# Windowed attention with sink keys, then a gated feed-forward layer: loads paced by use, more DMA transposes, and a fixed place for the sink-key copies

## The chip, the cores and the metric

The kernel runs on one core of one Trainium2 chip. The time is device microseconds (us) of one execution; of seven runs of the kernel before, the median is 254.44 us (253.92 to 255.36). The profile is of one execution; its times are counted from the start of its span.

## The reference

There are 4 batches of 8 heads, 768 positions and 64 elements a head. Each position attends to the 4 sink keys at the start and to the last 128 positions. The attention output, as 3072 rows of 512 elements, goes through a row normalisation and a gated feed-forward layer of width 1536.

```python
scores = scale * np.matmul(q, k.transpose(0, 1, 3, 2))
keep = is_sink | ((rel >= 0) & (rel < window))
a = softmax(np.where(keep, scores, -1e9))
x = np.matmul(a, v)                       # then rows of all heads side by side
xn = x / np.sqrt(np.mean(x * x, -1) + 1e-6) * rms_g
g = xn @ w_gate
out = (g * sigmoid(g) * (xn @ w_val)) @ w_out
```

## The kernel before

**Tiles.** The rows are cut into 24 blocks of 128 (NB), 6 to a batch. A block g of batch b and place t in the batch has q, k and v of all heads as bf16 tiles of 128x512, cast from fp32 by the DMA that loads them (`load_q`, `load_k`, `load_v`, issued by POOL, lines 111 and 124). q and k are then transposed into `QKT[b]`, a tile for a whole batch of which there are two. This is done either on PE (eight 128x128 transposes into PSUM, line 251, and a copy by ACT or DVE, lines 264 and 286), or by two DMA transposes issued by SP (line 278). Before, the DMA does it for blocks 13 to 17 and 19 to 23.

**One block's attention.** `unit_s(g)` makes the scores of the keys of block g with the queries of blocks g and g+1 (line 413; in the last block of a batch with its own alone), so it needs k of block g and q of g and g+1. ACT takes the exponential (line 422), and the mask is a multiplication on DVE (line 388) or, in batches 2 and 3 outside their first block, two selections on POOL (lines 390 and 395). `unit_sink(b)` prepares the sink keys of a batch: it clears a tile, copies 4 columns of the transposed k twice (64 partitions by 16 elements each, line 297, on DVE), and makes the sink values (lines 306 and 310). `unit_sink_scores` uses the copies (line 321) two blocks at a time. `unit_av(g, u)` multiplies by v for four heads (lines 444 to 456); DVE takes the reciprocal of the sums (line 479) and scales the output (line 484, `unit_norm`); ACT squares it (line 494); DVE works out the row factor (lines 503 to 525) and the scaled row (line 541). From block 8 on, the rows are transposed by a DMA of SP (line 549), before that on PE (line 563).

**Feed-forward.** Four blocks make a group G of 512 rows; there are six groups. For each of 12 slices of the width there is a gate product and a value product (line 581, four matmuls of 128x512 each), a tanh on ACT (line 594) and two DVE operations (lines 599 and 607). Then each block has 12 output matmuls (line 622), a copy by ACT (line 629) and a store by SP (line 631).

**Order.** The feed-forward parts of a group are woven with the attention units of the blocks ahead. `step(g)` gives four slots: the scores of g in slot 0, the output of g-1 in slots 1 and 3, the transposes in slot 2 (of block g+2 on PE, or of g+3 by DMA). `manual_schedule` makes the order in which the code is written binding for the engines that it names: in the main part PE and SP. For the others, a planner in the compiler sets the order from its own estimate of costs and readiness. All engines take their instructions in order. `tc.issue_after(ins)` puts the instructions of its block behind `ins` on the engine of `ins`; it adds no wait between engines.

**Loads.** POOL issues all loads: at first, in an order written out by hand, the weights and blocks 1 to 7, and then, behind the last of the weights, blocks 8 to 23. The pool `ld` has 18 buffers for q and 18 for k; v has a place of its own for every block. All PSUM tiles of the main part share eight banks.

Of the kernel before, what the change touches and what calls it, by code (L numbers as in the profile page):

```python
# [28 lines left out]
def kernel(  # L29
# [13 lines left out]
    nc = tc.nc  # L43
# [12 lines left out]
    GB = 4  # L56
# [6 lines left out]
    NEG = -32768.0  # L63
    RMS_EPS = 1e-6 * RSQRT_SCALE ** 2
    MS_SCALE = RSQRT_SCALE / math.sqrt(DM)
    DMA_T_FROM = 12

    DMA_X_FROM = 8
    FA = 10
    WEAVE_FROM = 9  # L70
    POOL_MASK_FROM = 2
    MANUAL = {mybir.EngineType.PE, mybir.EngineType.SP}
    MANUAL_ALL = MANUAL | {mybir.EngineType.Activation, mybir.EngineType.DVE}

    const = ctx.enter_context(tc.tile_pool(name="const", bufs=1))
    ld = ctx.enter_context(tc.tile_pool(name="ld", bufs=3 * NT))
    vld = ctx.enter_context(tc.tile_pool(name="vld", bufs=B))
    qkt = ctx.enter_context(tc.tile_pool(name="qkt", bufs=2))
    sink = ctx.enter_context(tc.tile_pool(name="sink", bufs=2))
# [36 lines left out]
    def load_q(g):  # L116
        QS[g] = load_block(q, "qs", g)

    def load_k(g):
        KS_[g] = load_block(k, "ks", g)  # L120

    def load_v(g):
        b, t = divmod(g, NT)
        nc.gpsimd.dma_start(  # L124
            out=V16[b][:, t, :, 0:D],
            in_=v[b, :, t * P:(t + 1) * P, :].rearrange("h t d -> t h d"),
        )
# [12 lines left out]
    def load_wo(c):  # L140
        rows = slice(c * FTN // 2, (c + 1) * FTN // 2)
        return nc.gpsimd.dma_start(out=wo[:, rows, :], in_=wo_src[:, rows, :]).ins
# [41 lines left out]
    with tc.manual_schedule(engines={mybir.EngineType.Pool, mybir.EngineType.DVE}):  # L184
        load_q(1)
        nc.gpsimd.affine_select(
            out=ident, in_=ident, compare_op=ALU.not_equal, fill=1.0,
            base=0, pattern=[[-1, P]], channel_multiplier=1,
        )
        nc.gpsimd.affine_select(  # L190
            out=amasks[:, 1, 0, :], in_=amasks[:, 1, 0, :], compare_op=ALU.is_ge,
            fill=NEG, base=0, pattern=[[1, P]], channel_multiplier=-1,
        )
        nc.vector.tensor_scalar(
            out=amasks[:, 1, 1, :], in0=amasks[:, 1, 0, :], scalar1=-1.0, scalar2=NEG,
            op0=ALU.mult, op1=ALU.add,
        )
        nc.vector.tensor_copy(out=amasks[:, 0, :, :], in_=amasks[:, 1, :, :])
        nc.vector.memset(amasks[0:NS, 0, :, :], 0.0)
        unit_cast(0)  # L200
        unit_cast(1)
        load_k(1)
        load_v(0)
        load_v(1)
        load_w(0)
        load_q(2)
        load_k(2)
        load_w(1)
        load_q(3)
        load_v(2)  # L210
        load_k(3)
        load_v(3)
        nc.gpsimd.affine_select(
            out=sel[:, 0:H * NS].rearrange("p (h s) -> p h s", s=NS),
            in_=sel[:, 0:H * NS].rearrange("p (h s) -> p h s", s=NS),
            compare_op=ALU.not_equal, fill=1.0,
            base=0, pattern=[[0, H], [-1, NS]], channel_multiplier=1,
        )
        nc.gpsimd.affine_select(
            out=headm, in_=headm, compare_op=ALU.is_ge, fill=0.0,  # L220
            base=0, pattern=[[-NS, H]], channel_multiplier=1,
        )
        nc.gpsimd.affine_select(
            out=headm, in_=headm, compare_op=ALU.is_ge, fill=0.0,
            base=NS - 1, pattern=[[NS, H]], channel_multiplier=-1,
        )
        load_w(2)
        load_w(3)
        load_q(4)
        load_w(4)  # L230
        load_k(4)
        load_w(5)
        load_v(4)
        for g in range(GB + 1, 2 * GB):
            load_q(g)
            load_k(g)
            load_v(g)
        load_wo(0)
        last_load = load_wo(1)
    with tc.issue_after(last_load):  # L240
        for g in range(2 * GB, NB):
            load_q(g)
            load_k(g)
            load_v(g)


    QKT, KSK, VSK, ESK, E, X16, MS, XR, XNT = {}, {}, {}, {}, {}, {}, {}, {}, {}
# [8 lines left out]
    def unit_t1(g, i):  # L256
# [9 lines left out]
            in_=ps[:, 0:HP * P].rearrange("p (x c) -> p x c", c=P),  # L266
        )

    def by_dma(g):
        return g >= DMA_T_FROM and g % NT > 0  # L270

    def unit_t(g):
        b, t = divmod(g, NT)
# [17 lines left out]
    def unit_sink(b):  # L291
        ks = sink.tile([P, HP * KSW], BF16, name="ksk")
        nc.vector.memset(ks, 0.0)
        ksv = ks.rearrange("p (h c) -> p h c", c=KSW)
        for hi in range(2):
            pr = slice(hi * D, (hi + 1) * D)
            nc.vector.tensor_copy(
                out=ksv[pr, :, hi * NS:(hi + 1) * NS],
                in_=QKT[b][pr, 1, :, 0:NS],
            )  # L300
        KSK[b] = ks
        vs = sink.tile([P, H, VW], BF16, name="vsk")
        for half in range(2):
            ps = pp[0].tile([P, 512], FP32, name="pvs", tag="b1")
            hs = slice(half * 4, half * 4 + 4)
            nc.tensor.matmul(
                out=ps[:, 0:HW], lhsT=sel, rhs=V16[b][:, 0, hs, :],
                start=True, stop=True,
            )
            nc.vector.tensor_tensor(  # L310
                out=vs[:, hs, :], in0=ps[:, 0:HW].rearrange("p (h c) -> p h c", c=VW),
                in1=headm[:, hs].unsqueeze(2).to_broadcast((P, 4, VW)), op=ALU.mult,
            )
        VSK[b] = vs
# [153 lines left out]
        if u == 1 and g >= 2:  # L468
            unit_rms(g)

    PV, RDEN = {}, {}

    def heads_of(g, u):

# [6 lines left out]
    def unit_norm(g, u, pvv):  # L481
        if (g, u) not in RDEN:
            unit_recip(g, u, pvv)
        nc.vector.tensor_tensor(  # L484
            out=X16[g][:, heads_of(g, u), :], in0=pvv[:, :, 0:D],
            in1=RDEN.pop((g, u)).unsqueeze(2).to_broadcast((P, 4, D)), op=ALU.mult,
        )

    def unit_sq(g, u):
        if u == 0:  # L490
# [145 lines left out]
    def step(g):  # L636


        b, t = divmod(g, NT)
        slots = [[], [], [], []]  # L640
        if g < NB:
            slots[0].append(lambda: unit_s(g))
            if t == 1:
                slots[1].append(lambda: unit_sink(b))
            if t in (2, 4):
                slots[1].append(lambda: unit_sink_scores(b, t))
        if g <= NB:
            slots[1].append(lambda: unit_av(g - 1, 0))
            slots[3].append(lambda: unit_av(g - 1, 1))
        if g - 3 < NB:  # L650
            slots[0].append(lambda: unit_x(g - 3))
        if g + 2 < NB and not by_dma(g + 2):
            slots[2 if t != 5 else 1].append(lambda: unit_t(g + 2))
        if g + 3 < NB and by_dma(g + 3):
            slots[2].append(lambda: unit_t(g + 3))
        return slots

    def weave(parts, slots, upto=0, first=False):
# [54 lines left out]

    with tc.manual_schedule(engines=MANUAL):


        fa, fb = [], []
        for ft in range(0, FA, 2):
            fa += parts_f(0, (ft, ft + 1), slice(0, GN // 2))
            fb += parts_f(0, (ft, ft + 1), slice(GN // 2, GN))  # L720
        for ft in range(FA, FTN):
            fb += parts_f(0, (ft,), slice(0, GN))
        weave(fa, [
            [lambda: unit_t1(2, 1), lambda: unit_bias(1, 1), lambda: unit_sp(1, 1), lambda: unit_sink(0)],
            [lambda: unit_t1(3, 0), lambda: unit_s(2)],
            [lambda: unit_sink_scores(0, 2)],
            [lambda: unit_t1(3, 1), lambda: unit_bias(3, 0), lambda: unit_av(2, 0), lambda: unit_sp(3, 0), lambda: unit_av(2, 1)],
            [lambda: unit_av(3, 0)],
            [lambda: unit_av(3, 1), lambda: unit_t1(4, 0)],
            [lambda: unit_bias(3, 1), lambda: unit_sp(3, 1)],  # L730
            [lambda: unit_x(2)],
            [lambda: unit_t1(4, 1)],
            [lambda: unit_x(3)],
        ], first=True)
        slots = [[lambda: unit_t1(5, 0)], [lambda: unit_t1(5, 1)], [lambda: unit_s(4)], [lambda: unit_sink_scores(0, 4)], [lambda: unit_t(6)], []]
        for g in range(5, NB + 3):
            slots += step(g)
        slots[6].pop()
        slots[10].pop()
        outs = []  # L740
        n = 0
        for G in range(NG):

            parts = fb if G == 0 else []
            for ft in range(FTN if G > 0 else 0):
                parts += parts_f(G, (ft,), slice(0, GN))
                if ft % 3 == 2 and outs:
                    parts += outs.pop(0)
            outs = [parts_o(G, tb) for tb in range(GB)]
            if G < WEAVE_FROM or G == NG - 1:  # L750
                for o in outs:
                    parts = parts + o
                outs = []
            n1 = 6 + 4 * ((G + 2) * GB + 2 - 5) + 1
            weave(parts, slots[n:n1], 1)
            n = n1
# [33 lines left out]
```

The softmax here doesn't subtract the row's maximum and nothing guards it: scores larger than these inputs give would overflow.

## Time and profile before

| | |
|---|---|
| median of 7 runs | 254.44 us |
| profiled execution, its time / its span | 254.44 / 252.7 us |
| PE busy | 240.4 us |
| DVE busy | 181.2 us |
| ACT busy | 139.4 us |
| POOL busy | 98.0 us |
| DMA packets / bytes | 105849 / 25.74 MB |
| loads of q, k, v: issue to landing, median | 7.7 to 7.8 us |
| DMA transposes, issue to landing, median | 2.4 us |

How to read it: the shares of the engines say how busy each was over the span; in the row of 40 slices, one digit is the busy share of 6.3 us in tenths. The chain of waits is followed back from the last instruction, at each step to what released it. A timeline row has start and duration in us, the engine, the line, the operation, output and inputs; in brackets the idle time of the engine before it and what ended it. Matmuls overlap, so their pitch (start to start) says what they cost and not their duration.

### The profile page before, as it was taken

The numbers are of one execution on the slowest core, as the hardware profiler recorded it, in microseconds if no ns is written. First come the engines' busy times: TensorE is split into PE (matmuls) and PEld (weight loads), VectorE is DVE, ScalarE is ACT, GpSimd is POOL, SyncE is SP. The second block draws the span as 40 slices with busy tenths as digits, with TensorE's granted clock in tenths as the row PEclk, the third lists the DMA queues.
The fourth block names the chain that finished last, engine by engine and source line by source line (L and its number), as shares of the span: only waits on it lengthen the run. The fifth ranks groups of instructions, "written<-read, shape, count | busy, mean of one in ns | idle before, by whom it ended". The sixth has DMA issues, their size and how long they took to land.

```text
span 252.7 us, 4804 instructions
## 1 busy us (share of the span) xinstructions
PE 240.4 (95%) x1733; PEld 128.5 (51%) x1760; DVE 181.2 (72%) x474; ACT 139.4 (55%) x312; POOL 98.0 (39%) x129
## 2 busy tenths in 40 slices
PE   5988989999999999999999999999999999999994
PEld 1436868855555444454454454454454544444441
DVE  5474897899778999539989459988359992287700
ACT  2576768789896365556473546466545441323211
POOL 8987779289985652134041004044201000000000
PEclk9999999999999999999999999999999999999999
DMA  9999999999999999750120550320421013200022
GB/s 128 150 171 191 188 157 189 185 155 151 179 198 171 150 127 150 125 172 18 21 52 14 145 145 3 64 56 18 117 84 23 0 21 95 94 0 0 0 86 83
DMA packets 105849, 25.74 MB, mean 102 GB/s; under 512 B 95073, under 2 KB 102753, under 8 KB 105826
## 3 DMA queue, kind: packets, MB, share of 16 engines
q0 software_dynamic: 80704, 13.90, 76.1%
q1 hardware_dynamic: 24082, 11.28, 18.9%
q10 hardware_dynamic: 1040, 0.26, 0.5%
q8 instruction: 14, 0.23, 0.4%
q14 instruction: 9, 0.07, 0.1%
HBM read 28.31 MB, written 6.29 MB: 137 GB/s over the span
## 4 chain that ended last, share of the span: by engine, by line
PE 79%; DVE 13%; ACT 4%; issue 2%; DMA 2%; ACTq 0%; DVEq 0%
PE po L622 24%; PE pg L581 20%; PE pvl L581 20%; PE pT L413 3%; DVE hT L607 3%; DVE p L599 3%; PE pv L456 2%; PE pqk L251 2%; DVE et L388 2%; PE pv L452 2%; DMA osb<-in_q_dram 2%; DVE xr L541 2%; PE pv L444 1%; ACT et L422 1%; PE pss L321 1%
## 5 line engine op out<-in xcount | busy, mean ns | idle before, releaser
L581 PE MATMUL pg<-xnt,wg 128*128 128x512 bf16 (+1 forms) x317 | 73.5, 352 | 1.4 <-ACT xnt L567 0.7
L581 PE MATMUL pvl<-xnt,wv 128*128 128x512 bf16 (+1 forms) x322 | 73.4, 353 | 0.3
L622 PE MATMUL po<-wo,hT 128*128 128x512 bf16 x279 | 64.9, 379 | 0.5 <-issue 0.2
L594 ACT ACTIVATE th<-pg 128x512 bf16<-128x512 f32 x72 | 42.9, 596 | 38.4 <-PE pg L581 38.4
L599 DVE SCALAR_TENSOR_TENSOR p<-th,pg 128x512 bf16<-128x512 bf16 x72 | 49.0, 680 | 20.0 <-ACT th L594 19.6
L607 DVE TENSOR_TENSOR hT<-p,pvl 128x512 bf16<-128x512 bf16 x72 | 49.3, 685 | 3.7 <-PE pg L581 0.5
L581 PEld LDWEIGHTS <-wg 128*128 128x128 bf16 x328 | 30.5, 98 | 27.4 <-issue 1.4
L581 PEld LDWEIGHTS <-wv 128*128 128x128 bf16 x328 | 30.4, 98 | 27.1 <-issue 1.1
L422 ACT ACTIVATE et<-pT 128x512 bf16<-128x512 f32 x76 | 39.7, 601 | 4.9 <-PE pT L413 4.7
L390 POOL TENSOR_SCALAR_AFFINE_SELECT et<-et 128x512 bf16<-128x512 bf16 x20 | 13.1, 658 | 74.2 <-ACT et L422 74.2
L622 PEld LDWEIGHTS <-hT 128*128 128x128 bf16 x288 | 26.6, 98 | 29.8 <-issue 0.8
L494 ACT ACTIVATE sq<-x 128x256 bf16<-128x256 bf16 x48 | 20.0, 417 | 27.1 <-DVE x L484 26.8
L629 ACT ACTIVATE osb<-po 128x512 f32<-128x512 f32 x24 | 14.4, 602 | 25.8 <-PE po L622 20.8
L111 POOL DMA_DIRECT2D ks<-in_k_dram x23 | 20.5, 891 | 8.2 <-DMA wo<-in_moe_w_out_dram 2.8
L111 POOL DMA_DIRECT2D qs<-in_q_dram x23 | 20.6, 897 | 7.7 <-PE pv L456 2.6
L124 POOL DMA_DIRECT2D v<-in_v_dram x24 | 21.5, 895 | 2.3 <-DMA wg<-in_moe_w_gate_dram 1.4
L484 DVE TENSOR_TENSOR x<-pv,rden 128x256 bf16<-128x256 f32 x48 | 20.2, 422 | 0.8
L541 DVE SCALAR_TENSOR_TENSOR xr<-x,y,gb 128x512 bf16<-128x512 bf16 (+1 forms) x25 | 19.9, 798 | 0.7
L479 DVE RECIPROCAL rden<-pv 128x4 f32<-128x4 f32 x48 | 8.4, 176 | 16.1 <-PE pv L456 15.9
L388 DVE TENSOR_TENSOR et<-et,masks 128x1024 bf16<-128x1024 bf16 (+1 forms) x22 | 13.8, 638 | 2.7 <-ACT et L422 2.7
L456 PE MATMUL pv<-v,et 128*128 128x65 bf16 x168 | 15.3, 193 | 0.0
L452 PE MATMUL pv<-v,et 128*128 128x65 bf16 x136 | 12.7, 193 | 0.0
(75 smaller groups left out, 217.0 us busy)
## 6 DMA issues: line engine op xcount, KB each, us to landing
out_dram<-osb SPq DMA_DIRECT2D x24, 256.0 KB, 2.1
v<-in_v_dram POOLq DMA_DIRECT2D x24, 128.0 KB, 7.8
qs<-in_q_dram POOLq DMA_DIRECT2D x23, 128.0 KB, 7.7
ks<-in_k_dram POOLq DMA_DIRECT2D x23, 128.0 KB, 7.7
wg<-in_moe_w_gate_dram POOLq DMA_DIRECT2D x6, 256.0 KB, 7.7
wv<-in_moe_w_val_dram POOLq DMA_DIRECT2D x6, 256.0 KB, 8.0
wo<-in_moe_w_out_dram POOLq DMA_DIRECT2D x2, 768.0 KB, 10.4
osb<-in_k_dram ACTq DMA_DIRECT2D x1, 256.0 KB, 4.8
```

Of the source, the lines that this page charges most:

```text
L111: nc.gpsimd.dma_start(out=tl, in_=src[b, :, t * P:(t + 1) * P, :].rearrange("h t d -> t h d"),)
L124: nc.gpsimd.dma_start(out=V16[b][:, t, :, 0:D], in_=v[b, :, t * P:(t + 1) * P, :].rearrange("h t d -> t h d"),)
L422: nc.scalar.activation(out=et[:, hi].rearrange("p j n c -> p (j n c)"), in_=banks[u][hi], func=ACT.Exp, scale=inv_sqrt_d,)
L456: nc.tensor.matmul(out=dest, lhsT=E[(g, h, 0)], rhs=V16[b][:, t, h, :], start=(t == 0), stop=True, skip_group_check=True,)
L484: nc.vector.tensor_tensor(out=X16[g][:, heads_of(g, u), :], in0=pvv[:, :, 0:D], in1=RDEN.pop((g, u)).unsqueeze(2).to_broadcast((P, 4, D)), ...
L494: nc.scalar.activation(out=sq, in_=xh, func=ACT.Square, scale=MS_SCALE, accum_out=MS[g][:, u:u + 1],)
L541: nc.vector.scalar_tensor_tensor(out=XR[g][-1], in0=x16[:, c], scalar=y[:, 4:5], in1=gb[:, c], op0=ALU.mult, op1=ALU.mult,)
L581: nc.tensor.matmul(out=ps[:, i * n:(i + 1) * n], lhsT=w_sb[:, kt, ft * P:(ft + 1) * P], rhs=XNT[G][:, kt, cols], start=(kt == 0), stop=(kt ...
L594: nc.scalar.activation(out=st["th"], in_=st["pg"], func=ACT.Tanh, scale=0.5)
L599: nc.vector.scalar_tensor_tensor(out=p1, in0=st["th"], scalar=1.0, in1=st["pg"], op0=ALU.add, op1=ALU.mult,)
L607: nc.vector.tensor_tensor(out=HT[key][:, i:i + n, cols], in0=p1.rearrange("p (n c) -> p n c", n=n), in1=pvl.rearrange("p (n c) -> p n c", ...
L622: nc.tensor.matmul(out=st["po"], lhsT=HT[(G, ft // 2)][:, ft % 2, tb * P:(tb + 1) * P], rhs=wo[:, ft, :], start=(ft == 0), stop=(ft == FTN ...
```

## The change

Three things are changed. The pool `ld` has 4 buffers each for q and k in place of 18, and POOL's order is now bound to the code as well: the loads of block g+6 stand in slot 2 of step g, those of blocks 8, 9 and 10 in the slots before step 5. The DMA transposes start at block 10 and take the first block of a batch too, so blocks 10, 11, 12 and 18 leave PE and ACT. The two copies of the sink keys are put behind the `unit_norm` written last before them.

```diff
-    DMA_T_FROM = 12
+    DMA_T_FROM = 10
+    LD = 4
+    AHEAD = 6
-    MANUAL = {mybir.EngineType.PE, mybir.EngineType.SP}
+    MANUAL = {mybir.EngineType.PE, mybir.EngineType.SP, mybir.EngineType.Pool}
-    ld = ctx.enter_context(tc.tile_pool(name="ld", bufs=3 * NT))
+    ld = ctx.enter_context(tc.tile_pool(name="ld", bufs=LD))
...
-        last_load = load_wo(1)
-    with tc.issue_after(last_load):
-        for g in range(2 * GB, NB):
-            load_q(g)
-            load_k(g)
-            load_v(g)
+        load_wo(1)
...
+    def unit_load(g):
+        load_q(g)
+        load_k(g)
+        load_v(g)
...
     def by_dma(g):
-        return g >= DMA_T_FROM and g % NT > 0
+        return g >= DMA_T_FROM
...
-        for hi in range(2):
-            pr = slice(hi * D, (hi + 1) * D)
-            nc.vector.tensor_copy(
+        with tc.issue_after(LAST[0]):
+            for hi in range(2):
+                pr = slice(hi * D, (hi + 1) * D)
+                nc.vector.tensor_copy(
...
-        nc.vector.tensor_tensor(
+        LAST[0] = nc.vector.tensor_tensor(
...
-        )
+        ).ins
...
+        if g + AHEAD < NB:
+            slots[2].append(lambda: unit_load(g + AHEAD))
...
-        slots = [[lambda: unit_t1(5, 0)], [lambda: unit_t1(5, 1)], [lambda: unit_s(4)], [lambda: unit_sink_scores(0, 4)], [lambda: unit_t(6)], []]
+        slots = [[lambda: unit_t1(5, 0)], [lambda: unit_t1(5, 1), lambda: unit_load(8)], [lambda: unit_s(4)], [lambda: unit_sink_scores(0, 4), lambda: unit_load(9)], [lambda: unit_t(6)], [lambda: unit_load(10)]]
```

More of the change, by code (lines that the diff above doesn't have):

```diff
@@ L294, in unit_sink @@
         ksv = ks.rearrange("p (h c) -> p h c", c=KSW)
-        for hi in range(2):
-            pr = slice(hi * D, (hi + 1) * D)
-            nc.vector.tensor_copy(
-                out=ksv[pr, :, hi * NS:(hi + 1) * NS],
-                in_=QKT[b][pr, 1, :, 0:NS],
-            )
+        with tc.issue_after(LAST[0]):
+            for hi in range(2):
+                pr = slice(hi * D, (hi + 1) * D)
+                nc.vector.tensor_copy(
+                    out=ksv[pr, :, hi * NS:(hi + 1) * NS],
+                    in_=QKT[b][pr, 1, :, 0:NS],
+                )
         KSK[b] = ks
@@ L469, in unit_av @@
             unit_rms(g)
-    PV, RDEN = {}, {}
+    PV, RDEN, LAST = {}, {}, [None]
     def heads_of(g, u):
@@ L483, in unit_norm @@
             unit_recip(g, u, pvv)
-        nc.vector.tensor_tensor(
+        LAST[0] = nc.vector.tensor_tensor(
             out=X16[g][:, heads_of(g, u), :], in0=pvv[:, :, 0:D],
             in1=RDEN.pop((g, u)).unsqueeze(2).to_broadcast((P, 4, D)), op=ALU.mult,
-        )
+        ).ins
     def unit_sq(g, u):
```

## The prediction

> **What bounds it now.** I read the engines' shares and slices first, then the chain of waits, then the busy times stage by stage.
>
> ```profile
> PE 240.4 (95%) x1733; PEld 128.5 (51%) x1760; DVE 181.2 (72%) x474; ACT 139.4 (55%) x312; POOL 98.0 (39%) x129
> ...
> PE   5988989999999999999999999999999999999994
> PEld 1436868855555444454454454454454544444441
> DVE  5474897899778999539989459988359992287700
> ...
> DMA  9999999999999999750120550320421013200022
> ...
> PE 79%; DVE 13%; ACT 4%; issue 2%; DMA 2%; ACTq 0%; DVEq 0%
> ```
>
> PE carries 79% of the chain; DMA is full up to about 105 us (slice 17) and light after. The stages (us; busy of PE, PEld, DVE, ACT, POOL; clock; DMA):
>
> ```profile
> 40.00:60.00 20.00, 19.25 (x207) 13.91 (x208) 18.65 (x50) 16.57 (x36) 14.23 (x18) 1.00 1.98 175
> 60.00:73.00 13.00, 12.89 (x119) 7.51 (x120) 9.91 (x37) 12.03 (x30) 12.20 (x14) 1.00 2.58 174
> 73.00:98.00 25.00, 24.79 (x182) 12.61 (x183) 23.33 (x61) 14.82 (x35) 14.01 (x17) 1.00 2.31 155
> ```
>
> From 60 us on PE starts one matmul behind the other at a granted clock of 1.00, so an instruction taken off PE there is time saved. Before 60 us DVE has the word: the chain's pieces from 49.4 to 59.5 us are all DVE but for gaps of at most 0.19 us, and PE's idle of 0.75 us in 40 to 60 is paid to it. These two facts carry the forecast.
>
> **PE transposes removed (blocks 10, 11, 12, 18): a gain of 1.78 us.** PE's timeline shows block 12's pair and the matmul after it:
>
> ```profile
> 75.27 0.39 PE L251 MATMUL pqk<-ident,qs 128*128 128x128 bf16 x4
> 75.50 0.39 PE L251 MATMUL pqk<-ident,ks 128*128 128x128 bf16 x4
> 75.72 1.03 PE L581 MATMUL pg<-xnt,wg 128*128 128x512 bf16 x4
> ```
>
> Eight transposes hold PE from 75.27 to 75.72, 0.45 us (0.056 each). The other three (62.20, 67.59, 129.81 us) give 0.44, 0.44, 0.45 by the same subtraction, where a missing record is filled with the pitch of its neighbours, 0.216. All four lie after 60 us, on the path: 1.78 us. The Trainium skill ("TensorE: Matmul & The Clock Gate", Part 4: PE-mode transpose) gives about 275 ns for one transpose in a kernel's context; by it the estimate would be 32 x 0.275 = 8.8 us. The row's pitch decides.
>
> The four ACT copies (L286, 1.01 us each) go too. Counted at nothing: PE waited for none after 60 us. The bound below: all of PE's visible idle in 40 to 98 us (0.75 + 0.11 + 0.21 = 1.07 us) goes with them.
>
> **DMA transposes added (8, on SP).** Each occupies SP about 1.2 to 2.2 us, and SP has room. What counts is landing, shown by line 278 before and after 100 us (the former first):
>
> ```profile
> DMA to landing us min/median/max: 7.3/8.1/9.5
> ```
> ```profile
> DMA to landing us min/median/max: 2.4/2.4/2.6
> ```
>
> For blocks 12 and 18 cover is wide: issued in steps 9 and 15, used by the scores of steps 11 and 17. Blocks 10 and 11 are tight. q of block 10 was issued at 45.93 and landed 9.9 us later, 55.8. Its transpose, first on SP, must land before the scores of block 9 (64.73, minus 0.44 of PE saved: 64.29): 8.5 us of cover. Block 11 stands on SP behind the first output store (62.73, about 0.5), so starts at 63.3 and is due at the scores of block 10 (70.23 - 0.88 = 69.35): 6.05 us. Which landing holds at 56 to 69 us? Loads issued at 52 to 64 landed in 6.6 to 6.7 us, those of 70 to 80 in about 11, while transposes took 8.1: scaled, 2.4 + 6.7/11 x (8.1 - 2.4) = 5.9 us. That fits both covers, the second barely; but loads have thinned by then, as load 14 waits for block 10. So I take 0, with ends 0 and +3.4 (rival 2). The k halves follow 1.3 us later and are due a step later (k of block 10 landed at 56.6, due at 69.35). What stands behind on SP: the second output store, due at about 65.6 and kept some 0.3 us by block 11's pair, and the row transpose of block 8 at 72.98, after block 12's pair is issued at about 66 to 69. Nobody waits for either by then.
>
> **Pacing (four buffers each of q and k, loads in POOL's program order).** A load waits until the block four earlier is transposed. Against before's issue times: q4 18.26 (needs block 0, about 6), q7 33.10 (22.4), q8 38.41 (30.8), q10 45.93 (41.2), q12 54.33 (51.2), q13 57.32 (56.7): nothing is held through block 13. Block 14 is the first held, by block 10's transpose, from 59.92 to about 62. From there load g stands in step g-6 in POOL's order, its buffers are freed by the transposes of step g-7, and it is used in step g-3: three steps, some 27 us at the 9 us between the scores at 79.62, 88.53 and 97.66, for 2.7 us of POOL's issues (3 x 0.9) and 7 to 11 us of landing. Behind a load on POOL stand the masks (L390, L395, about 2.5 us a step): 2.7 + 2.5 is less than the 9 us between scores. Masks are due a step later, so nothing is charged; if a mask came a whole step late PE would wait, and the 3.8 us left over in a step are what stands against it. Lighter DMA from 66 to 105 us gains nothing, as PE did not wait for it.
>
> One rule speaks against moving loads into 100 to 140 us, where DVE is busy. The Trainium skill ("SBUF — State Buffer", SBUF: two separate sides) says that descriptors of a POOL-issued DMA cannot be written while VectorE runs an operation that holds both ports; and, under the heading on the bandwidth-pool intuition, that a DMA of 620 ns then takes 3100. By that factor of 5 the estimate for three issues of 0.87 us would be 13 us, more than a step, and loads would fall behind. The rows of this case say otherwise: between 82 and 93 us, with DVE busy 9.67 of 10 us, issues still take 0.87 to 0.89.
>
> **Sink copies (L297) pinned behind the last scaled output.**
>
> ```profile
> L297 DVE COPY ksk<-qkT x8: 158/170/518, 8.3 to 132.9; 64x16 bf16<-64x16 bf16 x8
> ```
>
> Two per batch. Batch 0: at 8.26 to 8.95 (0.69 us) they filled DVE idle; now they come after 14.43, where DVE's chain to the first normalised rows has gaps of under 0.2 us, and PE waits 0.69 us for it at 16.44. Cost 0 (after 18.5, DVE idles 1.96 us) to 0.69; I take 0.2, nearer to the idle. Batch 1: from 43.39 (0.70) to behind 55.4:
>
> The first line below is the last scaled output of block 5, behind which they now stand; DVE is then busy without a gap to the second, the row scaling of block 6, whose end PE waits for in the third:
>
> ```profile
> 55.01 0.43 DVE L484 TENSOR_TENSOR x<-pv,rden 128x256 bf16<-128x256 f32 x1
> ...
> 58.76 0.74 DVE L541 SCALAR_TENSOR_TENSOR xr<-x,y,gb 128x512 bf16<-128x512 bf16 x1
> ```
> ```profile
> 59.55 0.23 PEld L563 LDWEIGHTS <-xr 128*128 128x128 bf16 x4 [0.41 <-DVE xr L541]
> ```
>
> So what is added between them moves PE. Their leaving 43.39 repays nothing, as DVE then waits 1.06 us for ACT at 47.69 in any case. Cost 0 (if the planner puts them past 59.5) to 0.70; I take 0.35, two at the median of 170 ns. Batch 2: from 76.96, in a stage with DVE 93% busy, to about 97, before a stretch with DVE half idle: 0. Batch 3: from 132.76 to about 152.6, ahead of a stretch where DVE is busy 11.32 of 12 us: 0 to 0.35; I take 0. All copies land well before the sink scores that read them (60.65, 109.70, 164.40).
>
> **Sum.** -1.78 + 0.20 + 0.35 = -1.23 us. The profiled run took 254.44, span 252.7 and 1.74 around it, which is also the median: 253.2.
>
> **Rivals.**
> 1. *Gain eaten by DVE.* Copies at their longest: 0.69 + 0.70 + 0.35 = 1.74, net 0: 254.4. For: DVE has the word up to 60 us. Against: median of 170 ns, and gaps nearby. 0.27.
> 2. *Slower: the first DMA transposes land late.* At 9.5 us q of block 10 is ready at 65.3 instead of 64.29 (+1.0), and block 11 at 72.8 instead of 69.35 + 1.0 (+2.4). 3.4 - 1.78 + 0.55 = +2.2: 256.6. It decides from landings of 6.05 us (block 11) and 8.5 us (block 10). For: 9.5 was seen in a full DMA, and pacing holds nothing before block 14, so this stretch is as full as before. Against: loads landed faster there. 0.20.
> 3. *More gain.* PE's idle of 40 to 98 us goes too, copies cost nothing: -1.78 - 1.07 = 251.6. For: ACT is 93% busy in 60 to 73 and loses two copies. Against: PE waits for DVE, not ACT. 0.08.
> 4. *Pacing does not pace* before 59 us: true by the times above; it has no price of its own and is part of 2.
>
> **Chances.** The forecast itself 0.45 (own range 252.5 to 253.6). A measurement tells about 0.3% here, 0.76 us: faster, below 253.68, 0.45 + 0.08 = 0.53; within, 0.27; slower, 0.20. Leaving out the far part of 2 and of 3, the range is 252.2 to 256.5.
>
> **What would show it.** Line 251 with 80 PE matmuls instead of 112; 36 + 8 DMA transposes; no PE idle before the scores of blocks 9 and 10 (if 1 us or more stands there, rival 2); copies of batch 1 near 55.5 and PE's wait before L563 grown by about 0.35 (if 0.7 or more, rival 1); DMA slices below 9 from about 65 us. It would be wrong if DVE's or ACT's order, set by the planner, changes elsewhere before 60 us.

## The result and the profile after

The change makes the kernel slower: 256.99 us (median of 27 runs, 255.0 to 259.72) against 254.91 for the kernel before on the same chips (64 runs), a ratio of 1.0059 with an interval of 1.0043 to 1.0076. Medians in this document are of all executions, and ratios of the fast ones alone (executions more than 1.5% above a kernel's fastest are left out), so this ratio, worth 1.5 us, is smaller than the two medians suggest. The forecast was 253.2, faster. The profiled execution took 257.5 us, its span is 255.8 (before 252.7).

The page of the kernel after, the rows that answer to those shown of before:

```profile
PE 238.3 (93%) x1702; PEld 126.4 (49%) x1728; DVE 180.7 (71%) x474; ACT 135.9 (53%) x308; POOL 98.3 (38%) x129
...
PE   5968989979969999999999999999999999999993
PEld 2437768845535454454455444454454544444441
DVE  5655896889857999538999459989349992287700
...
PEclk9979999999999999999999999999999999999999
DMA  9999999999999999599799991321321012200022
...
PE 66%; DMA 11%; DVE 9%; POOL 5%; ACT 5%; issue 3%; SPq 0%; POOLq 0%; ACTq 0%; DVEq 0%
```

PE has 2.1 us less work, as the removed transposes let one expect. But DMA's share of the chain of waits has gone from 2% to 11% (on the page, 8% are loads of k and 3% the transpose of a q): PE now waits for transfers. The same stretches as before (columns: us, busy of PE, PEld, DVE, ACT and POOL with counts, clock, DMA, GB/s):

```profile
40.00:60.00 20.00, 18.30 (x198) 13.43 (x198) 16.73 (x48) 15.59 (x33) 10.53 (x13) 1.00 1.84 164
60.00:73.00 13.00, 10.79 (x96) 5.68 (x95) 10.76 (x37) 9.77 (x27) 7.87 (x9) 1.00 1.81 103
73.00:98.00 25.00, 24.02 (x172) 12.31 (x176) 21.43 (x54) 14.37 (x33) 9.37 (x11) 1.00 1.82 158
```

In 60 to 73 us PE idles 2.21 us where it had idled 0.11, and in 73 to 98 us 0.98 where it had idled 0.21, at the same clock. PE's waits of the kernel after name the cause (total us, times, longest; two waits at the start, which before has too, are left out between the second and the third line):

```profile
PE pT L415 <- DMA qkT<-qs: 2.4, 1, 2.4
PE pxt L565 <- DVE xr L543: 1.8, 2, 1.4
...
PE pqk L247 <- DMA qs<-in_q_dram: 1.2, 2, 1.0
PE pqk L247 <- DMA ks<-in_k_dram: 1.0, 2, 0.6
```

Three of these four are new (line 565 is 563 of before, where the entry read 1.1 in all and 0.7 at the longest). The first is one wait, before the scores of block 10, in PE's timeline and in that of SP's queue:

```profile
73.83 0.61 PE L415 MATMUL pT<-qkT 64*128 64x256 bf16 x8 [2.42 <-DMA qkT<-qs]
```
```profile
65.02 0.38 SPq L633 DMA_DIRECT2D out_dram<-osb  x1
65.45 1.36 SPq L279 DMA_TRANSPOSE qkT<-qs  x1
66.86 1.29 SPq L279 DMA_TRANSPOSE qkT<-ks  x1
```

The cover of a transfer is the time from its issue until PE is ready to use it, and its landing the time from its issue until the data have arrived. PE was ready at 73.83 - 2.42 = 71.41; q of block 11 was issued at 65.45, so the cover was 5.96 us. Line 279's transposes issued in 55 to 64 us (block 10), then in 64 to 68.2 (block 11):

```profile
DMA to landing us min/median/max: 3.7/4.1/4.6
```
```profile
DMA to landing us min/median/max: 8.2/8.5/8.7
```

q landed after 8.2 us and PE went on 0.2 us later: 8.4 less 5.96 is the wait. Where the 2.72 us between the two kernels' last output matmuls came from can be read off the starts of the scores on PE (us):

| from, to | before | after | difference | what is in it |
|---|---|---|---|---|
| start to first gate product | 19.06 | 18.88 | -0.18 | |
| to the scores of block 6 | 29.24 | 29.89 | +0.65 | a wait for the load of block 5, 0.69 |
| to those of block 8 | 10.51 | 11.67 | +1.16 | waits for q and k of block 8, 1.03 + 0.56 |
| to those of block 9 | 5.92 | 5.87 | -0.05 | block 10's transposes gone (-0.44); sink copies of batch 1 |
| to those of block 10 | 5.50 | 7.52 | +2.02 | block 11's transposes gone (-0.44); the wait of 2.42 |
| to those of block 11 | 9.39 | 8.92 | -0.47 | block 12's transposes gone |
| block 11 to 16 | 45.40 | 45.40 | 0 | |
| block 16 to 17 | 10.01 | 9.56 | -0.45 | block 18's transposes gone |
| to the last output product | 114.01 | 114.05 | +0.04 | |

So the gain is there at each of the four places, 0.4 to 0.47 us a block once the wait and the copies are taken off. It is lost before block 11.

The first two losses, as far as the kept profiles show, go with the execution and not with the change. Waits of PE's transposes for the loads of block 5 or 8 stand in the ten profiles whose first gate product starts at 18.88 us or earlier, and in none of the six where it starts at 19.06 or later, and each group holds kernels with the load order of before and with that of after. e14 (below) is the same program as the kernel after up to the loads of block 12; it starts at 20.17 and has none. An execution that starts early waits for loads that a late one finds landed. Counted from the scores of block 8 to the end of the span, the kernel after takes 195.4 us and before 193.9: 1.5 us, as the ratio says.

### The profile page after: what moved, and what is told of

Read it like the earlier page. It is cut to its first block, busy times and chain, and to the rows that moved or that the text cites. A ratio compares the mean times of both kernels' runs of the same rounds, so it can differ in the third digit from the quotient of the medians.

```text
span 255.8 us, 4785 instructions
## 1 busy us (share of the span) xinstructions
PE 238.3 (93%) x1702; PEld 126.4 (49%) x1728; DVE 180.7 (71%) x474; ACT 135.9 (53%) x308; POOL 98.3 (38%) x129
## 4 chain that ended last, share of the span: by engine, by line
PE 66%; DMA 11%; DVE 9%; POOL 5%; ACT 5%; issue 3%; SPq 0%; POOLq 0%; ACTq 0%; DVEq 0%
PE po L624 20%; PE pg L583 18%; PE pvl L583 18%; DMA ks<-in_k_dram 8%; DMA qkT<-qs 3%; PE pT L415 3%; DVE p L601 2%; ACT et L424 2%; DVE hT L609 2%; PE pv L458 1%; POOL v L125 1%; PE pv L454 1%; PE pv L446 1%; POOL qs L112 1%; POOL ks L112 1%
## 5 line engine op out<-in xcount | busy, mean ns | idle before, releaser
L458 PE MATMUL pv<-v,et 128*128 128x65 bf16 x168 | 15.3, 193 | 0.0
L415 PE MATMUL pT<-qkT 64*128 64x256 bf16 (+1 forms) x168 | 12.0, 261 | 3.1 <-DMA qkT<-qs 2.4
```

What stands on the lines that cost most here:

```text
L415: nc.tensor.matmul(out=banks[u][hi][:, j * w:(j + 1) * w], lhsT=QKT[b][pr, 1, hp, t * P:(t + 1) * P], rhs=QKT[b][pr, 0, hp, t * P:t * P + ...
```

## The experiments

Ratios are to the kernel before on the same chip, with their intervals; 0.1% is 0.25 us.

| kernel | median us | ratio |
|---|---|---|
| e1 transposes alone | 267.12 | 1.0485 (1.0425 to 1.0544) |
| e2 pacing alone | 255.11 | 1.0003 (0.9981 to 1.0025) |
| e3 pinned copies alone | 255.74 | 1.0030 (1.0004 to 1.0056) |
| e4 after, DMA transposes from block 12 | 255.08 | 1.0002 (0.9976 to 1.0029) |
| e5 before, blocks 12 and 18 by DMA, copies of batches 2, 3 pinned | 254.30 | 0.9981 (0.9965 to 0.9997) |
| e6 after, nothing pinned | 273.36 | 1.0741 (1.0721 to 1.0762) |
| e7 after, copies of batches 2, 3 pinned | 254.14 | 0.9972 (0.9943 to 1.0001) |
| e8 after, DMA transposes a step earlier | 253.72 | 0.9960 (0.9939 to 0.9982) |
| e9 after, 3 load buffers | 257.32 | 1.0049 (1.0020 to 1.0079) |
| e13 after, 18 load buffers | 258.32 | 1.0104 (1.0059 to 1.0149) |
| e14 after, no load beside block 11's transposes | 256.08 | 1.0057 (1.0025 to 1.0088) |
| e12 before, load 8 earlier | 254.31 | 0.9984 (0.9969 to 1.0000) |
| e10 = e8 + e7's pin + load 8 earlier | 253.05 | 0.9920 (0.9899 to 0.9941) |
| e15 = e10 with 18 load buffers | 252.04 | 0.9908 (0.9887 to 0.9930) |

The theory to test: rival 2 of the prediction, block 11's transposes landing late, is the loss. The rival theories: the pinned copies (rival 1), or the loads that the new order of POOL shifted.

### One part at a time

e1 has only this of the diff, e2 only the lines of the loads (LD, AHEAD, MANUAL, unit_load), e3 only those of `issue_after`:

```diff
-    DMA_T_FROM = 12
+    DMA_T_FROM = 10
-        return g >= DMA_T_FROM and g % NT > 0
+        return g >= DMA_T_FROM
```

> The kernel before with the DMA transposes of all q and k from block 10, and nothing else of the change (loads with 18 buffers, copies not pinned). Three theories of the loss. Late landing: the transposes of blocks 10 and 11 share the DMA with the stream of loads, land after 6 to 9 us, and PE waits 1 to 4 us before the scores of block 9 or 10; against the gain of 1.8 us the time is 0 to 2 us above before. Held loads, or pinned copies: neither is in this kernel, so it shows the gain of 1.8 us alone, 0.7% below before, with no wait before those scores.

> The kernel before with the paced loads alone (four buffers, POOL's order bound to the code; the transposes of blocks 10, 11, 12 and 18 stay on PE, copies not pinned). Held loads: PE waits for the loads of block 5 (about 0.5 us) and block 8 (about 1.6 us) as in the kernel after, and the time is about 2 us above before. Late landing, or pinned copies: no such wait, within 0.5 us of before.

> The kernel before with the sink copies pinned alone. Pinned copies: the pair of batch 0 lengthens DVE's chain to the first normalised rows by 0.4 to 0.8 us, PE's idle before its first row transpose grows from 0.7 to about 1.4 us, in some runs the clock dips after it, and the time is 0.5 to 1.5 us above before. Late landing, or held loads: within 0.4 us of before.

e1 has the wait of the first theory, 2.61 us before the scores of block 10, though its loads are those of before:

```profile
72.80 0.61 PE L413 MATMUL pT<-qkT 64*128 64x256 bf16 x8 [2.61 <-DMA qkT<-qs]
```

But it took 12 us more than before, which no theory had. DVE's waits and timeline in e1 say why:

```profile
DVE ksk L297 <- DMA qkT<-ks: 11.7, 2, 8.0
```
```profile
77.36 0.34 DVE L297 COPY ksk<-qkT 64x16 bf16<-64x16 bf16 x2 [8.05 <-DMA qkT<-ks]
```

Left to the planner, the copies of the sink keys of batch 2 stand so early in DVE's order that block 12's k, which now comes by DMA, has not landed. DVE takes its instructions in order, so everything behind the copy stood still for 8.05 us (and 3.61 us at block 18); behind the first stall PE's granted clock was also down, 0.50 in 80 to 84 us. The pin is therefore no cost of its own in batches 2 and 3: it is what lets blocks 12 and 18 go by DMA at all. The pacing alone is worth nothing that can be measured. The pin alone costs 0.30%, 0.8 us (0.1 to 1.4), all of it in batches 0 and 1: from the scores of block 10 on, the distances between the starts of the scores in e3 are those of before within 0.01 us.

### Which blocks, and which pins

e4 puts `DMA_T_FROM = 12` into the kernel after. e6 takes `issue_after` out of it. e5 (from before) and e7 (from after) pin only where the first block of a batch comes by DMA:

```diff
-        with tc.issue_after(LAST[0]):
+        with tc.issue_after(LAST[0]) if b >= 2 else ExitStack():
```

> The kernel after with the DMA transposes from block 12 on in place of block 10; blocks 10 and 11 go back to PE, which costs 0.9 us there. Late landing: the wait of 2.4 us before the scores of block 10 goes, the time is about 1.5 us below that of the kernel after. Held loads, or pinned copies: about 0.9 us above the kernel after, since their waits stay.

> The kernel after with the copies not pinned. If the pin protects: DVE waits for block 12's and block 18's transposes as in the run of the transposes alone (8.0 and 3.7 us there), and the time is 6 to 11 us above the kernel after. If the pacing protects, or the pin is only a cost: no such wait, 0.9 us below the kernel after.

> The kernel before, with blocks 12 and 18 transposed by the DMA too, and the copies pinned for batches 2 and 3 alone; no pacing. If the pin is what keeps DVE from standing in front of an unfinished DMA transpose, and if only its early batches cost time: no wait of DVE on the transposes, 0.9 us less PE work, 0.3% below before. If it is the pacing that makes these transposes harmless: DVE or PE waits 3 to 8 us for block 12, and the time is 1 to 4% above before.

> The kernel after with the copies pinned for batches 2 and 3 alone. If the cost of the pin lies in batches 0 and 1 (the start, and the stretch where DVE has the word): 0.9 us below the kernel after, PE's idle before its first row transpose back at 0.7 us. If it lies in batches 2 and 3: equal to the kernel after.

e4 against the kernel after gives the price of blocks 10 and 11: 1.0059/1.0002, 0.57% or 1.5 us (0.7 to 2.2 by the two intervals), net of the 0.9 us that PE saves there. Its wait for `qkT<-qs` is gone. e5 gives the worth of blocks 12 and 18: 0.19%, 0.5 us (0.1 to 0.9; the starts of the scores show 0.45 twice). e6 repeats the stall of e1, longer, and at some 17 us above the kernel after it costs more than the 6 to 11 us expected:

```profile
DVE ksk L298 <- DMA qkT<-ks: 16.1, 2, 10.3
```

e7 is 0.87% under the kernel after, more than the pin costs alone. In its profile q of block 11 landed after 6.8 us instead of 8.2, and PE waited only 0.8 us for it; whether the missing pin has a part in that was not tested. The parts add up within the intervals: e3 (+0.30%), e2 (+0.03%) and e5 (-0.19%) make +0.14%, and e4, which has all three, shows +0.02%. Blocks 10 and 11 bring the rest of the +0.59%.

### Why block 11's transposes land late

e8 writes the DMA transposes one step earlier, which brings block 11's ahead of the first output store:

```diff
-        if g + 3 < NB and by_dma(g + 3):
-            slots[2].append(lambda: unit_t(g + 3))
+        if g + 4 < NB and by_dma(g + 4):
+            slots[2].append(lambda: unit_t(g + 4))
```

> The kernel after with every DMA transpose of q and k written one step earlier, so that block 11's stands on SP ahead of the first output store. If that place is what makes it late: it is issued when its load has landed, near 61 instead of 65.4 us, and the wait of 2.4 us before the scores of block 10 shrinks by at least 2 us; 2 us or more below the kernel after. If the full DMA alone decides: it lands as late as before, and the time is that of the kernel after.

In e8, SP's queue issues q of block 11 at 58.80 instead of 65.45, block 11's two transposes land after 2.5 to 3.1 us, and PE meets the scores of block 10 without a wait:

```profile
58.80 1.19 SPq L279 DMA_TRANSPOSE qkT<-qs  x1
```
```profile
69.41 0.61 PE L415 MATMUL pT<-qkT 64*128 64x256 bf16 x8
```

It is faster than both kernels. This moves the place and also avoids the loads: in the kernel after, the loads of block 12 are held until block 10's k is transposed, and then nine transfers go out one behind the other, 0.87 to 0.94 us each, beside block 11's transposes. POOL's timeline of the kernel after, the first three of the nine:

```profile
63.17 0.87 POOL L112 DMA_DIRECT2D qs<-in_q_dram  x1 [6.33 <-DMA qkT<-ks]
64.03 0.88 POOL L112 DMA_DIRECT2D ks<-in_k_dram  x1
64.90 0.89 POOL L125 DMA_DIRECT2D v<-in_v_dram  x1
```

e9 (`LD = 3`) and e13 (`LD = 3 * NT`, 18) vary that hold:

> The changed kernel with three buffers instead of four for loads of q and of k: loads are held longer and fewer are in flight. Theory (block 11's DMA transposes land after 8.5 us because nine loads that had been held are issued in one burst beside them, 63 to 71 us): if fewer loads stand beside them they land in 6 us or less and PE's wait before the scores of block 10 falls from 2.4 to under 0.5, 255 us. Rival (only the place behind the first output store decides, at 65 us): the wait stays at 2 us or more, 257. A third outcome is that loads 11 to 13 now come late themselves: over 257.5 with PE or SP waiting for qs or ks.

> The changed kernel with 18 buffers for loads of q and of k, as before has: loads keep their new place in the order of POOL, but none is held for a buffer. Theory (the hold makes the burst, and the burst delays block 11's transposes): loads 12 and 13 go out before 62 us, the transposes of block 11 at 63 to 66 us land in about 6 us, PE's wait falls from 2.4 to 0.5 or less, 255 us. Rival (traffic beside the transposes slows them wherever it comes from, and loads merely stand earlier): landing of 7 us or more, wait 1.5 us or more, 256 to 257.

The theory that the burst decides gained nothing from either. Block 11 landed after 8.1 to 8.4 us in e9 (PE's wait 2.3); but there nine loads still go out one behind the other, only earlier (59.73 to 67.09), so e9 does not separate the theories. In e13 no load was held, loads went out from 54.71 to 71.67 with pauses of at most 1.0 us, and block 11 landed after 8.7 to 8.8 (wait 3.0). What e13 does show is block 10. Nothing but the number of buffers differs from the kernel after, and its transposes in 55 to 59 us, now with loads 12 to 14 beside them (issued from 54.71 to 62.21), took the first of these; block 11's the second:

```profile
DMA to landing us min/median/max: 7.2/7.4/7.6
```
```profile
DMA to landing us min/median/max: 8.7/8.8/8.8
```

So a stream of loads slows them without any hold; the hold had only given block 10 a quiet stretch (4.1 us). e14 is the direct test: block 11's transposes keep their place on SP, and POOL first copies a column of them, before loads 12 to 14.

```diff
+    def unit_hold():
+        nc.gpsimd.tensor_copy(
+            out=held.rearrange("p (i c) -> p i c", c=1),
+            in_=QKT[1][:, :, 0, 5 * P:5 * P + 1],
+        )
...
+        if g == 8:
+            slots[2].append(unit_hold)
+            for n in (12, 13, 14):
+                slots[2].append(lambda n=n: unit_load(n))
-        if g + AHEAD < NB:
+        if g + AHEAD < NB and g not in (6, 7, 8):
```

> The changed kernel, with loads 12, 13 and 14 written behind the transposes of block 11 and held on POOL until these have landed (POOL copies one column of q and of k of block 11 to a spare tile first); the place of the transposes on SP is not touched. Theory (traffic of loads decides the landing, not the place): block 11's transposes, issued at about 65 us with no load beside them, land in 2.5 to 4 us, PE does not wait for them, and the time is 2.4 us below the changed kernel, 254 to 255 us, unless loads 12 to 14 are then late themselves. Rival (the place behind the output store decides): landing of 8 us and a wait of 2 us as before, 257.

POOL's copy in e14, ahead of load 12, SP's queue, the landing of the q transpose that line 286 issued in 64 to 66 us, and PE at the scores of block 10:

```profile
70.28 0.19 POOL L272 COPY held<-qkT 128x2 bf16<-128x2 bf16 x1 [15.32 <-DMA qkT<-ks]
```
```profile
64.39 0.38 SPq L640 DMA_DIRECT2D out_dram<-osb  x1
64.81 1.24 SPq L286 DMA_TRANSPOSE qkT<-qs  x1
```
```profile
DMA to landing us min/median/max: 2.5/2.5/2.5
```
```profile
70.71 0.61 PE L422 MATMUL pT<-qkT 64*128 64x256 bf16 x8
```

Same place behind the output store, no load beside: 2.5 us and no wait. The traffic of loads decides; that is shown. The time did not fall with it, as loads 12 to 14 are now themselves late: block 13's transposes, issued at 80.26 beside them, landed after 9.7 to 9.9 us, and PE waited 1.60 us before the scores of block 12.

```profile
90.27 0.61 PE L422 MATMUL pT<-qkT 64*128 64x256 bf16 x8 [1.60 <-DVE y L530]
```

The row names DVE, but q of block 13 landed after 9.9 us, at 80.26 + 9.9 = 90.16: it is the transfer again. 2.42 less 1.60 leaves 0.8 us, and from the scores of block 8 to the end of the span e14 takes 194.5 us against 195.4 of the kernel after; the intervals of the two ratios cannot tell so little apart.

### The remaining losses, and a better kernel

e12 puts load 8 ahead of the two loads of `wo` in the kernel before; e10 joins this, e8 and the pin of e7; e15 is e10 with 18 load buffers.

```diff
+        load_q(8)
+        load_k(8)
+        load_v(8)
         load_wo(0)
```

> The kernel before with load 8 ahead of the loads of wo and nothing else. Theory (PE's wait for q and k of block 8, 0.15 us in the profile of before, up to 1.6 in that of the pacing alone, is a matter of when the load is issued on POOL): 0.2 to 0.8 us below before, 254.1 to 254.7, no PE wait on a load of block 8. Rival (DMA is full until about 100 us, so what goes first pushes back what follows, wo or block 9): no gain, within 0.3 us of before, the wait moved to another load or to line 624's weights.

> The changed kernel with three repairs, one for each loss found so far: DMA transposes written one step earlier, sink copies pinned for batches 2 and 3 only, load 8 placed ahead of the loads of wo. Theory (three separate losses: late transpose of block 11, 2.4 us; pin of batches 0 and 1, about 0.9; late load 8, 0.5 to 1.6): the kernel with early transposes alone took 253.72, so 253.72 - 0.9 - 0.5 = about 252.3, no PE wait on DMA qkT, none on a load of block 8, PE's wait for line 565 at 13 to 17 us back to 0.7. Rival (one loss seen three times: whatever lets blocks 10 and 11 arrive earlier gains the same 2 to 3 us once): 253.5 to 254, as with the early transposes alone.

> The kernel with the three repairs (early transposes, pin for batches 2 and 3 only, load 8 early), with 18 buffers instead of 4 for loads of q and of k, so that no load is held. Theory (the hold keeps loads out of 57 to 62 us, and the early transposes profit from that quiet stretch): transposes of blocks 10 and 11 land in 7 to 9 us instead of 2.5 to 4.7, still within the longer cover of block 11 (about 9.5 us) but near its end: 253 to 254.5. Rival (the early place alone gives the gain): the same time as with 4 buffers, 253.05, within 0.3 us.

e12 has no wait for block 8 and gains 0.16% (0 to 0.31): at the edge of what can be told. e10 gains 0.8% on before, against 0.4% of e8, so the losses are at least in part separate; at 253.05 it fell short of the 252.3 expected of it. e15 is the same within the intervals, although its transposes of 55 to 62 us landed late again:

```profile
DMA to landing us min/median/max: 6.5/8.2/8.3
```

Block 11 is issued there at 59.34 and due at 68.43: 9.1 us of cover. The early place alone gives the gain; the hold of the loads is not needed for it. These two are the fastest kernels of the study.

## Why the forecast was wrong

The step that failed is the landing of block 11's transposes: "So I take 0, with ends 0 and +3.4". Of what it was made from, the cover held: predicted as 6.05 us, measured as 5.96. The landing did not: estimated at 5.9 us by scaling it with the landing of loads, measured at 8.2 to 8.7. The wait of 2.42 is what rival 2 had for block 11 (+2.4). The sentence that chose between the ends, "loads have thinned by then", was wrong too: nine loads went out in 63 to 71 us, and e14 against the kernel after shows that loads beside a transpose are the whole difference between 2.5 and 8.2 us. By the prediction's own times load 14 was to be held only to about 62 us, before block 11's transposes at 63.3, so nothing was thin there. The range seen in the full DMA before 100 us (7.3 to 9.5) was the row to take.

The other terms close the sum. With 2.42 in place of 0, and the pin at the 0.8 us of e3 in place of 0.55, it is -1.78 + 0.8 + 2.42 = +1.4 us, and the ratio says +1.5. Without the wait it is -1.0, and e8, which has no such wait, is 0.40% or 1.0 us below before. Rival 2's total of 256.6 lies close to the 256.99 measured partly by luck: it holds +1.0 for block 10, which did not come.

**Transposes off PE.** Right: 1.78 us predicted, 0.4 to 0.47 seen at each of the four places, some 1.7 in all; PE has 80 transposes in line 247, and 28 DMA transposes of q and k stand in line 279. The price of 275 ns each that the Trainium skill gives ("TensorE: Matmul & The Clock Gate", Part 4: PE-mode transpose) would have made the gain 8.8 us by estimate; the starts of the scores show under 2.

**ACT copies.** Counted at nothing: right, nothing more than PE's part shows between the scores of blocks 10 and 11 or 16 and 17.

**Block 10, 12 and 18.** Right on PE's side: block 10 landed in 3.7 to 4.6 us and was not waited for, so rival 2's +1.0 did not come. But "cover is wide" looked at PE's scores alone. The first reader of blocks 12 and 18 is the copy of the sink keys on DVE, and without the pin it costs 12 us (e1 against before) or 17 us (e6 against the kernel after). The prediction priced the pin as a cost and did not see what it covers.

**Pacing.** The time is right (e2: 1.0003), the reason in part wrong: the first load held is 12, not 14, and it is released just beside block 11's transposes. It waits for block 10's transposes, two places before it and not four; in e4, where PE makes these transposes, load 12 goes out at 56.60 and is not held. Why is not shown. e13 shows that this hold did not cause the loss. The rule on POOL's descriptors was rightly left aside: POOL's issues of e8 stay at 0.87 to 0.97 us also in the burst, and in the kernel after at 0.87 in 84 to 88 us, where DVE is busy all of the 4 us. Whether any of DVE's operations here is of the kind that this rule means was not tested.

**Pinned copies.** Batch 1 was predicted at 0.35; the stretch from the scores of block 8 to those of block 9 is 6.25 us in e3 and 5.92 in before, and 5.87 in the kernel after against 5.51 in e7: 0.33 and 0.36. Batch 0 was taken at 0.2 of a range of 0 to 0.69 and is larger. DVE's timeline after, with the copies inside the chain to the first normalised row:

```profile
12.23 0.15 DVE L505 SCALAR_TENSOR_TENSOR m<-ms 128x1 f32<-128x1 f32 x1
12.29 0.84 DVE L299 COPY ksk<-qkT 64x16 bf16<-64x16 bf16 x2
13.16 0.16 DVE L511 TENSOR_SCALAR y<-m 128x1 int32<-128x1 int32 x1
```

In all seven kernels that pin batch 0 PE's wait for that row is 0.93 to 1.46 us, and 0.69 to 0.72 in those that do not: 0.24 to 0.77 more, 0.50 in e3. The 0.33 and the 0.50 of e3 together fit its 0.8 us, where 0.55 was predicted.

**What was not in the sum.** PE also waited for the loads of blocks 5 and 8 (0.69 and 1.59 us). The load of block 8 had landed with no slack in before, where PE stood 0.15 us between its q and its k. These waits come and go: e2, whose time is that of before, has them, e13 with the same order of POOL has none, and e1 has them without any pacing. They go with an early start of the execution, as said under the table of starts, and not with the change; e12 bounds what an earlier load 8 gives by 0 to 0.31%.

## What to carry to other kernels

Price a DMA transpose by its landing in the stretch where it will run, with the loads that are in flight there, and not by the row from an empty stretch; where the cover is within the range that was seen, write it a step earlier, which here cost nothing and turned +0.6% into -0.4%. When a producer is moved from an engine to the DMA, look up its first reader on every in-order engine, above all the small ones that a planner has placed: one pair of copies, 0.35 us, stopped VectorE for 8 to 10 us. Pin such a reader only where it needs it.

## What the runs showed of the hardware

The DMA transposes of q of block 11 (128x512) landed in 2.5 us with no load beside (e14) and in 8.1 to 8.8 us beside loads issued by another engine (the kernel after, e9, e13; 6.8 us in e7). The Trainium skill ("DMA: Bandwidth & Descriptors", Issuing engines are not separate DMA queues) says that transfers of all issuing engines share the same 16 DMA engines and interleave; these runs agree, and put a factor of 3.2 to 3.5 on it (2.7 in e7).

A wait of 2.3 to 3.0 us can cost PE more than its length: behind it the granted clock was 0.50 until some 3.5 us after the wait's end in e9 and e13. Stretches of e9 after its wait, which ended at 72.40, and of e13 (its wait ended at 74.27); the clock is the third column from the end:

```profile
70.00:74.00 4.00, 1.50 (x13) 0.95 (x14) 1.74 (x9) 2.12 (x7) 0.88 (x1) 0.83 1.84 170
74.00:78.00 4.00, 4.00 (x24) 2.00 (x24) 2.02 (x5) 2.23 (x5) 2.39 (x3) 0.74 1.60 196
```
```profile
74.00:78.00 4.00, 3.51 (x18) 1.80 (x20) 1.39 (x2) 2.54 (x5) 0.88 (x1) 0.57 1.81 166
```

From the scores of block 10 to those of block 11 they take 10.55 and 10.56 us, against 8.92 in the kernel after, whose wait of 2.42 us left the clock at 1.00: 1.6 us on top. The length of the wait alone does not decide: in e4 waits of 1.42 and 0.58 us, 0.4 us apart, were followed by a clock of 0.50 in 55 to 57 us, and the 1.60 us of e14 by none. That the wide spread of the kernel after (255.0 to 259.72) comes from this is likely and was not shown; of its 27 executions, the eight with a mean clock of 0.987 or less have a median of 257.9 us, the other nineteen one of 256.1. The Trainium skill ("TensorE: Matmul & The Clock Gate", Part 1: The HAM clock gate) puts the drop after an idle window of about 3.4 us; here 2.28 us was enough in e9 and 2.42 us was not in the kernel after. A lower clock (0.66 to 0.74) also stands at 15 to 20 us in half of the profiles, with and without the longer wait for the first row, so it does not need the pin.
